# kv and kv with Wo per head on 32-column and 32 by 32 TensorE tiles, and Wo loaded in 8 pieces after the row of z

## The chip, the cores and the metric

One core of one Trainium2 chip (trn2). The metric is device time of one execution, in microseconds; the profile is one execution of the same kernel, and its span (829.4 us before) is a little shorter than the timed runs (830.83 us). All runs that are compared here are listed as fast in the record.

## The reference, cut to what matters

A transformer block with adaptive layer norm, linear attention (S = 2048, D = 1024, 32 heads of 32) and a gated feed-forward part.

```python
q, k, v = split_heads(h @ wqkv)                     # h: (2048, 1024), 32 heads of 32
pq, pk = phi(q), phi(k)
kv  = einsum('bhsd,bhse->bhde', pk, v)              # one 32 x 32 matrix per head
z   = einsum('bhsd->bhd', pk)
num = einsum('bhqd,bhde->bhqe', pq, kv)
den = einsum('bhqd,bhd->bhq', pq, z)[..., None] + 1e-06
x   = x + ga * ((num / den) @ wo)
# ... then layer norm and the feed-forward part, about 580 of the 830 us
```

The kernel reorders this. It forms `G = h^T pk` (h transposed times pk), then `kv = Wv^T G`, of which only the 32 by 32 block of each head on the diagonal counts, then `M = kv Wo` per head, and at the end one product of the scaled pq with M. The change touches kv, M and the load of Wo.

## The kernel before: the parts that matter

Tiles have fixed places in on-chip memory. Each engine runs its operations in the order in which they are recorded. All loads below go through the queue of SyncE ("SP"), also in order.

```python
P.dma("wo", WO[:], wov)                     # wov = A_wo as (kt p) n -> p kt n : one 2 MB load
G_BANKS = [0] + [next_bank() for _ in range(4)]         # five PSUM banks for the G groups

def z_row():                                # z as a row in DRAM, fetched back to all partitions (ZB)
    ...
    zw = P.dma("zw", ZDR..., ZR8[0:NHG, :])
    P.wait_for("sp", [zw])
    P.dma("zr", ZB[:], ZDR[0:1, :].to_broadcast([128, D]))

def den():                                  # denominators: 32 matmuls on 32-column tiles
    for hg in range(NHG):
        for ch in range(NCH):
            P.pe("matmul", out=PS[32*ch:32*ch+32, 7, :], lhsT=ZSEL[:, hg*32:hg*32+32], ...)
    ...                                     # reciprocal, written to DRAM (recip_den) in 4 stores,
    P.wait_for("sp", wr)                    # then 8 broadcast loads into RB, each 512 KB
    ...

def scale_pq(hg):                           # VectorE; waits for RB
    P.dve("tensor_tensor", out=PQT[:, hg, :], in0=PQT[:, hg, :], in1=RB[:, hg, :], op=ALU.mult)

def kvt_mm(half):                           # 32 matmuls 128x128, of each only the diagonal is kept
    for hl in range(4):
        hg = 4 * half + hl
        for dt in range(NDT):
            P.pe("matmul", out=PS[:, 6, hl*128:(hl+1)*128], lhsT=WV[:, dt, hg*128:(hg+1)*128],
                 rhs=G[:, dt, hg*128:(hg+1)*128], ...)
    P.dve("tensor_tensor", out=KVT[:, 4*half:4*half+4, :], in0=PS[:, 6, :]..., in1=MASK..., op=ALU.mult)

def m_mm(hg, banks):                        # 2 matmuls 128x512, evicted by ACT and DVE
    ...

for g in range(16):
    g_group(g)                              # 16 matmuls 128x512, 3.45 us
    ...                                     # g_evac: bank -> G (needs ZB); one group behind
    if g == 0: z_row()
    if g == 1: ...; den()
    if 6 <= g <= 9: ...                     # fold ga into WO (VectorE)
    if g == 10: kvt_mm(0)                   # needs the evictions of groups 0 to 7
    if 11 <= g < 15: m_mm(g - 11, [MB, 7])
    if 7 <= g < 15: scale_pq(g - 7)         # VectorE, in order with the evictions
    if g == 10: P.dma("stgx1", ...)         # 2 MB of w_mod
g_evac(15)
P.dma("stgx2", ...)                         # 2 MB of w_mod
...                                         # 4 + 3 reloads of x (xr0 .. xr6)
wo_part(0, 0, range(4)); wo_part(0, 1, range(2)); kvt_mm(1); wo_part(...); m_mm(4, ...); ...
for st in range(NST): ...                   # output projection with M (MW)
```

## Time and profile before

| | before |
|---|---|
| time, median of 4 | 830.83 us (830.82 to 831.24) |
| TensorE busy | 823.2 of 829.4 us |
| kv: 2 blocks of 32 matmuls 128x128 | 1.79 us each |
| kv with Wo: 16 matmuls 128x512 | 0.216 us each, 3.46 us |
| Wo load: issue, landing | 131.35 us, 9.2 us later |

The page's first part gives the busy time of each engine (PE is TensorE's matmuls, PEld its weight loads), its share of the span and the instruction count:

```profile
PE 823.2 (99%) x4083; PEld 378.8 (46%) x4083; DVE 312.6 (38%) x665; ACT 197.5 (24%) x336; POOL 39.9 (5%) x57
```

The timeline of PE in the stage of the change. Columns: start in us, duration from the first start to the last end, engine, line, operation, output and inputs, shape, count; a bracket at the end would name idle time and what ended it. Since matmuls overlap (a 128x512 one is listed with 0.379 us, and the next starts 0.216 us after it), the difference of two starts is the time a group really takes.

```profile
133.79 1.91 PE L176 MATMUL ps<-pqt,zsel 128*32 128x512 bf16 x32
135.63 31.25 PE L176 MATMUL ps<-pk,xres 128*128 128x512 bf16 x144
166.72 1.95 PE L176 MATMUL ps<-g,wv 128*128 128x128 bf16 x32
168.51 3.62 PE L176 MATMUL ps<-pk,xres 128*128 128x512 bf16 x16
171.96 0.59 PE L176 MATMUL ps<-wo,kvt 128*128 128x512 bf16 x2
...
187.50 1.46 PE L176 MATMUL ps<-mw,pqt 128*128 128x512 bf16 x6
188.80 1.95 PE L176 MATMUL ps<-g,wv 128*128 128x128 bf16 x32
...
194.47 5.78 PE L176 MATMUL ps<-mw,pqt 128*128 128x512 bf16 x26
```

No line has a bracket: PE never idles here. Read 168.51 - 166.72 = 1.79 us for a kv block (`ps<-g,wv`). The first line is the denominator step, already on 32-column tiles: 32 matmuls of 512 columns in 135.63 - 133.79 = 1.84 us, in rounds of four that start 3 to 4 ns apart, with 0.205 to 0.216 us to the next round, so four run at a time.

The timeline of SP's queue, the order in which transfers were issued (duration is that of the issuing, not of the transfer):

```profile
131.35 1.29 SPq L176 DMA_DIRECT2D wo<-in_A_wo_dram  x1
132.68 0.53 SPq L176 DMA_DIRECT2D z_row<-zr  x1
140.08 0.33 SPq L176 DMA_DIRECT2D zb<-z_row  x1
141.62 2.93 SPq L176 DMA_DIRECT2D recip_den<-rcb  x4
145.89 4.07 SPq L945 DMA_DIRECT2D rb<-recip_den  x8
```

The small store of z (4 KB) takes from 132.68 until its wait ends at 140.08 us, because 2 MB of Wo are on the way (in the changed kernel, without Wo ahead of it, from 131.02 to 133.77 us). The line of VectorE's timeline that receives rb, with the one after it:

```profile
157.77 1.23 DVE L176 TENSOR_TENSOR pqt<-pqt,rb 128x2048 bf16<-128x2048 bf16 x1 [2.71 <-DMA rb<-recip_den]
158.92 0.74 DVE L176 SCALAR_TENSOR_TENSOR g<-ps,modcol,gtmp 128x512 bf16<-128x512 f32 x1
```

VectorE waited 2.71 us for rb. It does its work in order, so the eviction of G's group 7 (copying the product G out of its PSUM bank), the next in its order, is held back by the same wait. It ends at 159.66 us and the kv block that needs it starts at 166.72 us, so seven microseconds are left.

### The profile page before, as it was taken

The page shows a single profiled execution, that of the slowest core. Times are in us where ns is not written, and L with a number is a line of the kernel's source. Part 1 is how long each engine was busy: PE and PEld are TensorE (multiplying, and loading weights), DVE is VectorE, ACT ScalarE, POOL GpSimd, SP SyncE. Part 2 cuts the span into 40 slices and gives each one's busy share as a digit, 9 for nine tenths or more (in the row PEclk, how much of TensorE's full clock was granted, in tenths as well). Part 3 has the DMA queues.
Part 4 walks back from the last instruction along what each step waited for, and adds up shares of the span by engine and source line. Part 5 has one row for each costly group of instructions (what it writes and reads, how often), then busy time and mean ns, then how long its engine had stood idle before and what let it go on. Part 6 is the DMA issues. An engine that isn't in the chain of part 4 may idle for free.

```text
span 829.4 us, 10017 instructions
## 1 busy us (share of the span) xinstructions
PE 823.2 (99%) x4083; PEld 378.8 (46%) x4083; DVE 312.6 (38%) x665; ACT 197.5 (24%) x336; POOL 39.9 (5%) x57
## 2 busy tenths in 40 slices
PE   8999999999999999999999999999999999999998
PEld 4544444444444444444444444444444444444444
DVE  5797986756955521121221112122111211221111
ACT  4757641323242111011111101111110111111011
POOL 1010000000130000030000003000000300000000
PEclk9999999999999999999999999999999999999999
DMA  9969656938397985700455571045557004553000
GB/s 321 287 151 231 148 159 171 201 104 304 60 256 229 276 264 158 192 25 15 124 155 150 153 185 33 16 124 153 154 151 190 26 18 123 154 152 87 0 26 26
DMA packets 199246, 119.28 MB, mean 144 GB/s; under 512 B 57881, under 2 KB 182945, under 8 KB 199201
## 3 DMA queue, kind: packets, MB, share of 16 engines
q1 hardware_dynamic: 199184, 118.65, 52.8%
q8 instruction: 32, 0.52, 0.3%
q14 instruction: 14, 0.11, 0.0%
q10 hardware_dynamic: 16, 0.00, 0.0%
HBM read 100.67 MB, written 4.33 MB: 127 GB/s over the span
## 4 chain that ended last, share of the span: by engine, by line
PE 97%; DMA 2%; SPq 1%; issue 0%; DVE 0%
PE ps L176 97%; DMA wsa<-in_w_mod_dram 2%; SPq L176 1%; DVE xres L176 0%
## 5 line engine op out<-in xcount | busy, mean ns | idle before, releaser
L176 PE MATMUL ps<-h2t,gug 128*128 128x512 bf16 x896 | 211.7, 379 | 0.0
L176 PE MATMUL ps<-h2t,guu 128*128 128x512 bf16 x896 | 211.7, 379 | 0.0
L176 DVE TENSOR_TENSOR at<-sg,ps 128x512 bf16<-128x512 bf16 x112 | 77.0, 687 | 282.8 <-PE ps L176 281.2
L176 ACT ACTIVATE sg<-ps 128x512 bf16<-128x512 f32 x112 | 66.9, 597 | 309.7 <-PE ps L176 309.7
L176 PEld LDWEIGHTS ps<-h2t,guu 128*128 128x128 bf16 x896 | 87.6, 98 | 105.7
L176 PEld LDWEIGHTS ps<-h2t,gug 128*128 128x128 bf16 x896 | 87.7, 98 | 105.5
L176 PE MATMUL ps<-wd_a,at 128*128 128x512 bf16 (+1 forms) x512 | 112.4, 377 | 0.0
L176 PE MATMUL ps<-ht,wqk 128*128 128x512 bf16 x512 | 111.7, 379 | 0.0
L176 PE MATMUL ps<-wd_b,at 128*128 128x512 bf16 (+1 forms) x384 | 85.0, 377 | 0.0
L176 PEld LDWEIGHTS ps<-wd_a,at 128*128 128x128 bf16 x512 | 50.1, 98 | 59.6
L176 DVE TENSOR_TENSOR ut<-att,gb_b 128x512 bf16<-128x512 bf16 (+1 forms) x32 | 14.3, 447 | 166.8 <-ACT att L176 166.8
L176 PEld LDWEIGHTS ps<-ht,wqk 128*128 128x128 bf16 x512 | 49.5, 98 | 58.7 <-DVE biasq L176 0.2
L176 ACT ACTIVATE att<-ps 128x512 bf16<-128x512 f32 (+1 forms) x32 | 17.4, 591 | 182.1 <-PE ps L176 182.1
L176 PEld LDWEIGHTS ps<-wd_b,at 128*128 128x128 bf16 x384 | 37.6, 98 | 44.7
L176 PE MATMUL ps<-pk,xres 128*128 128x512 bf16 x256 | 56.5, 379 | 0.0
L176 PE MATMUL ps<-mw,pqt 128*128 128x512 bf16 x256 | 56.3, 379 | 0.0
L176 POOL TENSOR_SCALAR h2t<-h2t,modcol 128x512 bf16<-128x512 bf16 x32 | 26.3, 836 | 383.4 <-DMA h2t<-xn 383.4
L176 ACT ACTIVATE e<-ps 128x512 bf16<-128x512 f32 x56 | 33.1, 603 | 31.7 <-PE ps L176 19.8
L176 PEld LDWEIGHTS ps<-mw,pqt 128*128 128x128 bf16 x256 | 24.9, 98 | 30.2 <-DVE xres L176 0.4
L176 PEld LDWEIGHTS ps<-pk,xres 128*128 128x128 bf16 x256 | 24.9, 98 | 29.9 <-issue 0.4
L176 ACT ACTIVATE junk<-xres 128x1024 bf16<-128x1024 bf16 x24 | 25.4, 1058 | 35.1 <-DVE xres L176 34.9
L176 DVE SCALAR_TENSOR_TENSOR xres<-ps,xres 128x512 bf16<-128x512 f32 x32 | 21.4, 688 | 12.3 <-PE ps L176 11.5
(107 smaller groups left out, 344.8 us busy)
## 6 DMA issues: line engine op xcount, KB each, us to landing
gug<-in_B_w_gate_dram SPq DMA_DIRECT2D x56, 512.0 KB, 4.0
guu<-in_B_w_up_dram SPq DMA_DIRECT2D x56, 512.0 KB, 5.3
xres<-in_A_x_dram SPq DMA_DIRECT2D x20, 256.0 KB, 7.7
rb<-recip_den SPq DMA_DIRECT2D x8, 512.0 KB, 11.5
stgx<-in_w_mod_dram SPq DMA_DIRECT2D x2, 2048.0 KB, 7.9
wd_a<-in_B_w_down_dram SPq DMA_DIRECT2D x4, 1024.0 KB, 7.8
out_dram<-xres SPq DMA_DIRECT2D x31, 128.0 KB, 1.7
xres<-in_A_x_dram SPq DMA_DIRECT2D x3, 1024.0 KB, 14.1
```

Source lines behind the costliest of these rows:

```text
L176: return getattr(e, method)(**kw)
```

## The change

Intent: of each 128 by 128 product only four 32 by 32 diagonal blocks are wanted. On 32-column tiles the four heads of a group are computed one beside the other, without the masked rest; for kv with Wo, sixteen 32 by 32 tiles work on sixteen heads at once (measured below: starts 3 to 4 ns apart in a round of four, and 2 to 5 ns apart for the sixteen). For the second step a head's kv sits on the partitions of its group `g`, and the kernel takes the rows of Wo from the same partitions, so they are reordered: row `(f g h e)` goes to partition `32 g + e`, slot `4 f + h`. One load per `(f, h)` does that, eight in all. They are issued after the fetch of the row of z, so that z no longer waits behind Wo.

```diff
-        KVT = T("kvt", 188 * KB, [128, NHG, 128], BF16)
+        KVT = T("kvt", 188 * KB, [128, 2, 128], BF16)
-        wov = A_wo.rearrange("(kt p) n -> p kt n", p=128)
+        wov = A_wo.rearrange("(f g h e) n -> f h g e n", f=2, g=4, h=4)
-        P.dma("wo", WO[:], wov)
         def kvt_mm(half):
-            for hl in range(4):
-                hg = 4 * half + hl
+            for h in range(4):
                 for dt in range(NDT):
-                    P.pe("matmul", out=PS[:, 6, hl * 128:(hl + 1) * 128], lhsT=WV[:, dt, hg * 128:(hg + 1) * 128],
-                         rhs=G[:, dt, hg * 128:(hg + 1) * 128], start=(hl == 0 and dt == 0), stop=(dt == NDT - 1),
+                    for g in range(4):
+                        c0 = 512 * half + 128 * g + 32 * h
+                        P.pe("matmul", out=PS[32 * g:32 * g + 32, 6, 32 * h:32 * h + 32], lhsT=WV[:, dt, c0:c0 + 32],
+                             rhs=G[:, dt, c0:c0 + 32], start=(h == 0 and dt == 0), stop=(dt == NDT - 1),
                          skip_group_check=True)
-            P.dve("tensor_tensor", out=KVT[:, 4 * half:4 * half + 4, :], ... MASK ...)
+            P.dve("tensor_copy", out=KVT[:, half, :], in_=PS[:, 6, 0:128])
-        def m_mm(hg, banks):  ...  # 2 matmuls 128x512
+        def m_mm(half, nh, banks):
+            for k in range(4):
+                for g in range(4):
+                    h = (g + k) % 4
+                    P.pe("matmul", out=PS[32 * h:32 * h + 32, banks[g], :],
+                         lhsT=KVT[32 * g:32 * g + 32, half, 32 * h:32 * h + 32],
+                         rhs=WO[32 * g:32 * g + 32, 4 * half + h, nh * 512:(nh + 1) * 512], start=True, stop=True,
+                         skip_group_check=True)
...                                           # four evictions per block, ACT and DVE in turn
             if g == 0:
                 z_row()
+                for f in range(2):
+                    for h in range(4):
+                        P.dma("wo%d%d" % (f, h), WO[:, 4 * f + h, :], wov[f, h])
...                                           # m_mm in 4 blocks instead of 8 pairs, banks, order of wo_part
```

More of the change, by code (lines that the diff above doesn't have):

```diff
@@ L904, in g_group @@
             h, dt = g // NDT, g % NDT
-            bank = G_BANKS[g % 5]
+            bank = G_BANKS[1 if g == 14 else g % 5]
             for st in range(NST):
@@ L911, in g_evac @@
             h, dt = g // NDT, g % NDT
-            bank = G_BANKS[g % 5]
+            bank = G_BANKS[1 if g == 14 else g % 5]
             i = g % 2
@@ L952, in kvt_mm @@
         def kvt_mm(half):
-            for hl in range(4):
-                hg = 4 * half + hl
+            for h in range(4):
                 for dt in range(NDT):
-                    P.pe("matmul", out=PS[:, 6, hl * 128:(hl + 1) * 128], lhsT=WV[:, dt, hg * 128:(hg + 1) * 128],
-                         rhs=G[:, dt, hg * 128:(hg + 1) * 128], start=(hl == 0 and dt == 0), stop=(dt == NDT - 1),
-                         skip_group_check=True)
-            P.dve("tensor_tensor", out=KVT[:, 4 * half:4 * half + 4, :],
-                  in0=PS[:, 6, :].rearrange("p (g d) -> p g d", g=4),
-                  in1=MASK[:].unsqueeze(1).to_broadcast([128, 4, 128]), op=ALU.mult)
@@ L963, in bass_adaLN_cond__linear_attn_block__swiglu_ffn__prompt_kernel @@
-        m_ctr = [0]
-        def m_mm(hg, banks):
-            for nh in range(2):
-                i = m_ctr[0]
-                m_ctr[0] += 1
-                bank = banks[i % len(banks)]
-                P.pe("matmul", out=PS[:, bank, :], lhsT=KVT[:, hg, :], rhs=WO[:, hg, nh * 512:(nh + 1) * 512],
-                     start=True, stop=True)
-                dst = MW[:, hg, nh * 512:(nh + 1) * 512]
-                if i % 2 == 0:
-                    P.act("activation", out=dst, in_=PS[:, bank, :], func=ACT.Copy)
+                    for g in range(4):
[3 more added lines that the diff above has]
+                             skip_group_check=True)
@@ new lines, in kvt_mm @@
+            P.dve("tensor_copy", out=KVT[:, half, :], in_=PS[:, 6, 0:128])
[6 more added lines that the diff above has]
+                         rhs=WO[32 * g:32 * g + 32, 4 * half + h, nh * 512:(nh + 1) * 512], start=True, stop=True,
+                         skip_group_check=True)
+            for g in range(4):
+                dst = MW[:, 4 * half + g, nh * 512:(nh + 1) * 512]
+                if g % 2 == 0:
+                    P.act("activation", out=dst, in_=PS[:, banks[g], :], func=ACT.Copy)
@@ L975, in m_mm @@
                 else:
-                    P.dve("tensor_copy", out=dst, in_=PS[:, bank, :])
+                    P.dve("tensor_copy", out=dst, in_=PS[:, banks[g], :])
         def fold_ga(jt):
@@ L1011, in bass_adaLN_cond__linear_attn_block__swiglu_ffn__prompt_kernel @@
                 kvt_mm(0)
-            if 11 <= g < 15:
-                m_mm(g - 11, [MB, 7])
+            if 11 <= g < 13:
+                m_mm(0, g - 11, [MB, 7, G_BANKS[4], 6])
             if 7 <= g < 15:
@@ L1025, in bass_adaLN_cond__linear_attn_block__swiglu_ffn__prompt_kernel @@
         wo_part(0, 1, range(2, 4))
-        wo_part(1, 0, range(3))
-        m_mm(4, [4, 5, 7, 6])
-        wo_part(1, 0, (3,))
-        wo_part(1, 1, (0,))
-        m_mm(5, [4, 5, 7, 6])
-        wo_part(1, 1, range(1, 3))
-        m_mm(6, [4, 5, 7, 6])
-        wo_part(1, 1, (3,))
-        m_mm(7, [4, 5, 7, 6])
+        wo_part(1, 0, range(1))
+        m_mm(1, 0, [4, 5, 7, 6])
+        wo_part(1, 0, range(1, 4))
+        wo_part(1, 1, range(4))
+        m_mm(1, 1, [4, 5, 7, 6])
         for ch in range(1, NCH):
@@ L1076, in bass_adaLN_cond__linear_attn_block__swiglu_ffn__prompt_kernel @@
         for st in range(NST):
-            for nh in range(2):
-                wo_part(st, nh, range(4, 8) if st < 2 else range(8))
-                wo_res(st, nh)
+            for (sw, nh) in (((0, 0), (1, 0)), ((0, 1), (1, 1)))[st] if st < 2 else ((st, 0), (st, 1)):
+                wo_part(sw, nh, range(4, 8) if st < 2 else range(8))
+                wo_res(sw, nh)
             if st >= 1:
```

## The prediction

> **What bounds it now.** TensorE. The page shows PE busy 823.2 of 829.4 us; the chain of waits that ended last is 97% PE. In the timeline of PE from 128 to 200 us no idle gap appears: a 128x512 matmul starts every 0.216 us, a 128x128 one every 0.056. Only PE work, or a new PE stall, can move the time; DVE (38%), ACT (24%) and DMA have slack.
>
> **What the change removes, adds, moves (128 to 200 us only).**
> 1. kv. Before: 2 blocks of 32 matmuls 128x128, 1.79 us each (timeline). After: 2 blocks of 128 matmuls on 32-column tiles, four at a time. The denominator step already runs in this mode: its start times show four 128x512 matmuls 3 to 4 ns apart, then 0.206 to 0.216 us to the next four, so four column tiles run together. The shortest spacing of weight load plus matmul on one tile here is 25 ns (the one-column matmuls at 10 to 27 us). 32 rounds of four give 0.8 us if tiles overlap as there; 3.2 us if instructions cannot pass faster than 25 ns per pair. The trace holds no long stream of short tiled matmuls: this is the weak term. Estimate: 1.2 us.
> 2. kv with Wo. Before: 16 full matmuls, 3.46 us. After: 4 blocks of 16 on 32 by 32 tiles. [...] nothing in this trace has 32-row tiles. Estimate per block: 0.216 + 16 x 4 ns = 0.28 us, against 0.86 before.
> 3. Mode switches. [...] into the denominator block the start gap is 0.309 us instead of 0.216, out of it 0.312; about 0.2 us the round trip. Six new blocks: 1.2 us.
> 4. VectorE: the masked 128x512 KVT product (0.69 us, twice) becomes a 128x128 copy. Off the chain, but PE awaits the second KVT, and only three matmuls (0.65 us) now stand behind the kv block instead of five. Reuse of the four banks between the last two Wo blocks is tight too (1.5 us of matmuls, about 1.5 us of evictions). Estimate 0.2 us of new stalls.
> 5. Wo loads. The row of z no longer queues behind 2 MB of Wo (zb landed at 144 us), so the G evictions start earlier; rb may land a little later (DVE waited 2.7 us for it). PE waited for neither before. Worth 0.
>
> **Sum.** kv: 2 x (1.2 - 1.79) = -1.2. Wo: 4 x (0.28 - 0.86) = -2.3. Switches +1.2, stalls +0.2. Total -2.1 us, all on the critical path: 830.83 becomes 828.8 us. Range 827.4 to 831.4. Faster by over 2%: 0.01; within: 0.98; slower: 0.01.
>
> **What would show each step.** PE timeline: a kv block of 0.8 to 1.5 us, starts of a round 4 ns apart; a Wo block of about 0.3 us; gaps of 0.3 us at each change of tile shape; no PE wait over 0.3 us on KVT, MW or banks; G evictions starting near 138 to 140 us; everything after 200 us only shifted.
>
> **What would make it wrong.** Instruction issue limits the short matmuls (a kv block of 2 us or more: gain gone). 32 by 32 tiles run four at a time, not 16 (a Wo block of 0.86 us: +2.3). [...] A late rb or Wo holding VectorE so long that G's banks come free late.

## More of the kernel before

A recording layer notes which operation reads and writes what and adds waits; it compares columns only, not partitions.

The reciprocals (`recip_den`) go out at 141.6 and rb from 145.9 us.

## The result, and the profile after

The changed kernel took 840.1 us (median of 4, 839.65 to 841.63) against 830.83 us, so it is 9.3 us slower; the ratio is 1.0114 (95% interval 1.0096 to 1.0131), inside the 2% that count as the same. Ratios here are the mean time of one kernel's fast runs over that of the other's fast runs of the same rounds, so they are not quite the ratio of the medians.

The page after, busy time first: PE did a little less work in a longer span.

```profile
PE 822.5 (98%) x4323; PEld 376.7 (45%) x4323; DVE 310.9 (37%) x665; ACT 197.4 (24%) x336; POOL 39.9 (5%) x57
```

PE's timeline of the same stage:

```profile
135.32 31.25 PE L176 MATMUL ps<-pk,xres 128*128 128x512 bf16 x144
166.50 0.38 PE L176 MATMUL ps<-g,wv 128*32 128x32 bf16 x28
173.46 0.99 PE L176 MATMUL ps<-g,wv 128*32 128x32 bf16 x100 [6.58 <-DVE g L176]
174.38 5.10 PE L176 MATMUL ps<-pk,xres 128*128 128x512 bf16 x16
179.56 0.44 PE L176 MATMUL ps<-wo,kvt 32*32 32x512 bf16 x16
179.93 1.04 PE L176 MATMUL ps<-pk,xres 128*128 128x512 bf16 x4
182.65 2.75 PE L176 MATMUL ps<-pk,xres 128*128 128x512 bf16 x12 [1.69 <-issue]
...
196.07 1.46 PE L176 MATMUL ps<-mw,pqt 128*128 128x512 bf16 x6
197.46 1.19 PE L176 MATMUL ps<-g,wv 128*32 128x32 bf16 x128
...
201.69 1.04 PE L176 MATMUL ps<-mw,pqt 128*128 128x512 bf16 x4
203.81 11.38 PE L176 MATMUL ps<-mw,pqt 128*128 128x512 bf16 x52 [1.09 <-issue]
```

Three gaps are new. The first, 6.58 us in the middle of the first kv block, ends with an eviction of G by VectorE. The 16 matmuls after it take 5.1 us instead of 3.6: the first eight start 0.40 to 0.43 us apart. The other two gaps have the releaser "issue", which means that no semaphore explains them. The tiled blocks themselves are short, as intended.

Followed back from the first gap, the chain leads to the queue of loads. SP's timeline:

```profile
131.02 1.21 SPq L176 DMA_DIRECT2D z_row<-zr  x1
...
134.15 13.36 SPq L176 DMA_DIRECT2D wo<-in_A_wo_dram  x8
147.56 3.91 SPq L176 DMA_DIRECT2D recip_den<-rcb  x4
159.61 4.04 SPq L944 DMA_DIRECT2D rb<-recip_den  x8
```

Issuing the eight Wo loads took 13.36 us. The reciprocals went out at 147.56 instead of 141.62 us, and were confirmed 12 us later instead of 4, so rb started at 159.6 instead of 145.9 us. VectorE shows what that did:

```profile
171.43 1.23 DVE L176 TENSOR_TENSOR pqt<-pqt,rb 128x2048 bf16<-128x2048 bf16 x1 [16.68 <-DMA rb<-recip_den]
172.57 0.75 DVE L176 SCALAR_TENSOR_TENSOR g<-ps,modcol,gtmp 128x512 bf16<-128x512 f32 x1
```

It sat 16.68 us in front of `scale_pq(0)`, and the eviction of G's group 7, next in its order, came at 172.57 instead of 158.92 us. PE's kv block wanted it at 166.7 us.

Why the loads were slow is seen in two stretches of the windows view of the changed kernel (columns: stretch in us; its length; busy time and number of instructions on PE, PEld, DVE, ACT, POOL; granted clock; mean busy share of the 16 DMA engines; GB/s):

```profile
134.00:148.00 14.00, 14.00 (x87) 6.25 (x80) 10.24 (x12) 4.81 (x7) 0.00 (x0) 1.00 0.31 115
148.00:160.00 12.00, 12.00 (x58) 5.45 (x56) 3.90 (x6) 1.44 (x2) 0.00 (x0) 1.00 0.26 97
```

While Wo was loading, the mean busy share was about a quarter and the engines moved about 100 GB/s. The trace's semaphore updates say the same: each of the changed kernel's Wo loads reported five times, one update at issue and four as data landed, while the one load of before reported sixteen times. Four landings and a share of 0.26 of the 16 engines (4 of 16 would be 0.25) say that a load ran on four of them. The slowest dimension of these loads is `g`, of size 4; that of the load of before is `p`, of size 128. That its size sets the number of engines is the author's estimate from these two; experiment 1 adds a load with 32 there.

The reciprocals' updates show who was waiting for whom. The first of their four stores reported twelve landings at 150.95 to 151.12 us, about 1 us after its issue ended, and the last four only at 158.53 to 159.00 us, each 0.2 us after one of the four landings of the last Wo load (158.35 to 158.83). So three quarters of that store were through at once, and by these times the last quarter stood behind Wo.

### Where the 8.8 us of this stage went

From the two timelines, as differences of start times:

| term | us |
|---|---|
| gap inside the first kv block (starts at 166.69 and 173.46) | +6.76 |
| matmuls at half clock afterwards (8 matmuls in 3.21 instead of 1.73, 174.38 to 177.59) | +1.48 |
| "issue" gap at 182.65 (2.07 between starts instead of 0.216) | +1.85 |
| "issue" gap at 203.81 (1.47 instead of 0.216) | +1.25 |
| longer wait for KVT before the first Wo block | +0.15 |
| what is left: the tiled blocks themselves | -2.70 |
| measured for the stage: (203.81 - 135.32) - (195.33 - 135.63) | +8.79 |

(195.33 is the kernel before at the same point, four matmuls after 194.47.) The last term is a remainder, not a measurement, and needs its own test: if it is right, the tiles are worth 2.7 us once the gaps are gone.

The half clock is in the windows view too: the granted clock was 1.00 in the first 3.6 us of the gap (166.88 to 170.50 us), 0.51 from 170.50 to 177.40, and 1.00 from there to 200. So in this run the clock fell some 3.6 us into the gap of 6.6 us and was back some 3.9 us after PE resumed at 173.46.

### The profile page after: what moved, and what is told of

Same layout as the page of the kernel before. It is cut to its first block, busy times and chain, and to the rows that moved or that the text cites. A ratio compares the mean times of both kernels' runs of the same rounds, so it can differ in the third digit from the quotient of the medians.

```text
span 837.8 us, 10508 instructions
## 1 busy us (share of the span) xinstructions
PE 822.5 (98%) x4323; PEld 376.7 (45%) x4323; DVE 310.9 (37%) x665; ACT 197.4 (24%) x336; POOL 39.9 (5%) x57
## 4 chain that ended last, share of the span: by engine, by line
PE 87%; DVE 5%; DMA 4%; SPq 2%; issue 1%; ACT 0%; DVEq 0%; ACTq 0%
PE ps L176 87%; DVE acc L176 2%; SPq L176 2%; DMA rb<-recip_den 1%; DMA stg<-in_w_mod_dram 1%; DMA recip_den<-rcb 1%; DVE pqt L176 1%; DVE pkt L176 1%; DVE e L176 1%; DMA xres<-in_A_x_dram 0%; DVE mhl L176 0%; DMA z_row<-zr 0%; DVE wo L176 0%; DVE g L176 0%; DVE stats L176 0%
## 5 line engine op out<-in xcount | busy, mean ns | idle before, releaser
L176 PEld LDWEIGHTS ps<-mw,pqt 128*128 128x128 bf16 x256 | 24.7, 98 | 31.4 <-issue 1.8
## 6 DMA issues: line engine op xcount, KB each, us to landing
xres<-in_A_x_dram SPq DMA_DIRECT2D x3, 1024.0 KB, 13.7
```

The lines of the kernel that those rows point to most:

```text
L176: return getattr(e, method)(**kw)
```

## The experiments

Theory A: the loss is the Wo load on 4 DMA engines, which holds back the reciprocals and rb, then VectorE, then PE. Rival B: eight loads at this place are bad however they are cut. Rival C: the tiled matmuls, their banks or changes of mode hold PE.

### 1. Wo cut by 32 partitions, in the changed kernel

```diff
-        wov = A_wo.rearrange("(f g h e) n -> f h g e n", f=2, g=4, h=4)
+        wov = A_wo.rearrange("(f g h e) n -> f g e h n", f=2, g=4, h=4)
-                        P.dma("wo%d%d" % (f, h), WO[:, 4 * f + h, :], wov[f, h])
+                        P.dma("wo%d%d" % (f, h), WO[32 * h:32 * h + 32, 4 * f:4 * f + 4, :], wov[f, h])
```

> The changed kernel, with its 8 loads of Wo (256 KB each, 2 KB rows, same place in the queue) cut by groups of 32 partitions, so that the slowest dimension of a load is 32 instead of 4. Theory A (a load whose slowest dimension is 4 runs on 4 of the 16 DMA engines, at 101 GB/s as the trace shows, and the write of the reciprocals queues behind it): each Wo load is issued in about 0.5 us instead of 1.7, Wo lands by 146 us, the reciprocals land by 147 us instead of 159.5, rb's first half by 159 us, VectorE waits under 4 us for rb instead of 16.7, PE has no 6.6 us stall before the first kv block; time 827.5 to 831. Rival B (any 8 loads at this place delay the chain) and rival C (the tiled matmuls or their banks hold PE): time stays at 838 or more. If the two instruction-fetch gaps of 1.7 and 1.1 us are there by themselves, at least one stays, and the time is nearer 831.

Measured: 839.43 us (before in the same rounds 831.20; ratio 1.0098), correct. This looks like a refutation of theory A, and it is a failed experiment instead. SP's timeline:

```profile
135.59 20.89 SPq L176 DMA_DIRECT2D wo<-in_A_wo_dram  x8
156.52 1.82 SPq L176 DMA_DIRECT2D recip_den<-rcb  x4
```

Each load now reported 16 landings, so the 16 engines were used, and a load was through about 3 us after its issue. But six of the eight were issued only when the one before had landed: SP's list of waits has 18.0 us, in six waits, for Wo itself. Loads to partitions 0 to 31 and 32 to 63 of the same columns look like overlapping writes to the recording layer, which compares columns only, and it chained them. The reciprocals left at 156.5 us, later still, and rb began at 159.9 us, as in the changed kernel, with the same loss (gap of 5.3 us in the first kv block). What it does show is that the loss follows the time at which the reciprocals are through, whatever holds them back.

### 2. The kernel before with eight late loads, and with the 4-row loads

Eight loads of 128 rows in the old layout, issued at the changed kernel's place:

```diff
-        P.dma("wo", WO[:], wov)
             if g == 0:
                 z_row()
+                for i in range(NHG):
+                    P.dma("wo%d" % i, WO[:, i, :], wov[:, i, :])
```

> The kernel before with its one load of Wo replaced by 8 loads of 128 rows in its own layout (slowest dimension 128), issued where the changed kernel issues them, after the fetch of the row of z. Theory A: harmless, 830.5 to 831.5 us, no PE stall; rb at most 2 us later than before. Rival B: 836 us or more.

Measured: 831.52 us against 831.20 (ratio 1.0002, 0.9987 to 1.0017). The eight issues took 4.20 us and the reciprocals left at 140.59 us, so eight loads at this place need not hurt. Rival B falls.

The same with `wov = A_wo.rearrange("(f g h e) n -> f h g e n", ...)`, so the loads of the changed kernel under the matmuls of before (the result is wrong in its values, not in the amount of work):

> Wrong result on purpose (rows of Wo in the changed kernel's order under the matmuls of before). The kernel before, with the changed kernel's 8 loads of Wo (slowest dimension 4) at the changed kernel's place, and all matmuls of before. Theory A: the loss appears without any tiled matmul: Wo loads 2.5 us apart, reciprocals landed at about 159 us, PE stalled some 6 to 7 us before the first kv block, then slow clock; time 838 to 840 us. Rival C (tiled matmuls): 831 us.

Measured: 839.99 us against 831.20 (ratio 1.0107, 1.0092 to 1.0122). (The comparison with the reference doesn't see an attention term with permuted rows; the time is what counts here.) SP and PE:

```profile
134.51 13.98 SPq L176 DMA_DIRECT2D wo<-in_A_wo_dram  x8
```

```profile
174.20 2.80 PE L176 MATMUL ps<-g,wv 128*128 128x128 bf16 x25 [6.88 <-DVE g L176]
```

The whole gap appears without a single new tile. Rival C falls for this gap: the layout of the loads alone makes it.

### 3. Wo cut by 32 partitions, not chained

Four loads are recorded as one operation, so nothing is put between them:

```diff
+                    outs = [WO[32 * g_:32 * g_ + 32, 4 * f:4 * f + 4, :] for g_ in range(4)]
+                    ins = [wov[f, g_] for g_ in range(4)]
+                    def fn(e, outs=outs, ins=ins):
+                        return [e.dma_start(out=o_, in_=i_) for o_, i_ in zip(outs, ins)]
+                    P.add("sp", fn, reads=[], writes=outs, lane="wo%d" % f, ninc=4, tag="wo")
```

> The cut by 32 partitions again. In the run before it each load waited for the one before to land, because the recording layer takes loads to different partitions of the same columns for overlapping; here four loads go out as one operation, so they are not chained. Theory A (what delays the reciprocals is that Wo occupies the queue and its engines until about 159 us; on 16 engines and unchained it is gone by 145 us): reciprocals landed by 147 us, rb's halves at 151 and 161 us, no PE stall of 5 to 7 us before the first kv block; time 827.5 to 831, the lower end if the two fetch gaps (1.7 and 1.1 us) vanish too, since the rb traffic is over by then, the upper end if they stay. If time stays at 838 or more, theory A is wrong and the tiled blocks themselves are to blame.

Measured: 830.26 us against 831.06 (ratio 0.9987, 0.9970 to 1.0004). About ten microseconds came back from cutting the same 2 MB of Wo differently. SP's queue:

```profile
134.90 4.54 SPq L1006 DMA_DIRECT2D wo<-in_A_wo_dram  x8
141.74 1.71 SPq L176 DMA_DIRECT2D recip_den<-rcb  x4
150.30 4.19 SPq L944 DMA_DIRECT2D rb<-recip_den  x8
```

Rb started 4 us later than before but early enough: VectorE waited 6.74 us for it, and PE didn't wait. Two times of the expectation were missed by some 3 us: Wo landed at 148.63 us, not 145, and the reciprocals at 150.22, not 147. PE:

```profile
186.79 1.46 PE L176 MATMUL ps<-mw,pqt 128*128 128x512 bf16 x6
188.18 1.19 PE L176 MATMUL ps<-g,wv 128*32 128x32 bf16 x128
189.30 0.82 PE L176 MATMUL ps<-mw,pqt 128*128 128x512 bf16 x3
190.06 0.43 PE L176 MATMUL ps<-wo,kvt 32*32 32x512 bf16 x16
190.42 1.68 PE L176 MATMUL ps<-mw,pqt 128*128 128x512 bf16 x7
...
192.40 1.04 PE L176 MATMUL ps<-mw,pqt 128*128 128x512 bf16 x4
195.09 20.23 PE L176 MATMUL ps<-mw,pqt 128*128 128x512 bf16 x93 [1.65 <-issue]
```

Here the tiles can be priced. The second kv block costs 189.30 - 186.79 less six matmuls of 0.216, so 1.21 us with both changes of mode (before: 1.79). A Wo block costs 190.42 - 189.30 less three matmuls, so 0.47 us with its changes of mode (before: 0.86). Together 2 x 0.58 + 4 x 0.39 = 2.7 us, the remainder of the balance above. But one of the "issue" gaps is still there and eats 1.65 us of it (the profile is of the slowest of the four runs, 830.93 us).

### 4. What the "issue" gap is

The trace shows the packets that bring instructions: one of 16,384 bytes for each 256 instructions of PE (32 packets for 8,166 matmuls and weight loads in the kernel before, 34 for 8,646 in the changed one). In the feed-forward part, from 298 us on, these packets start when PE is at number 152 to 172 of each 256 in the trace's order in the kernel before, and at 153 to 180 in the changed one. The "issue" gaps lie at numbers 2241 and 2753 in the changed kernel and at 2753 in the version of experiment 3, so at number 193 of a 256. That suggested theory F: these are edges of instruction blocks; a block is asked for when the one before it is entered; the request waits behind data traffic; and a kv block, which is 256 instructions in 1.1 us instead of the 28 us that 256 take at 0.216 us per pair, uses up the lead. Times around the gaps (from PE's instruction numbers and the packets' start times; "due" is the author's estimate, worked out from the edge one block before, since the trace shows the packets but no requests):

| version | edge | due | packet starts | PE runs on at |
|---|---|---|---|---|
| changed kernel | 2241 | about 173.5 | 179.91 | 182.65 |
| changed kernel | 2753 | about 197.8 | 201.35 | 203.81 |
| experiment 3 | 2753 | about 188.5 | 192.73 | 195.09 |

A packet takes 1.0 to 1.3 us and PE ran on 2.4 to 2.7 us after its start. Rival G: PE waits there for a bank, an eviction or the reload of x, and the profile misses the semaphore.

Three versions of experiment 3 and a control, on one chip. First, 144 more PE instructions at the start and nothing else, which moves all block edges against the program:

```diff
-        warm(13, bank=3)                  # 13 warm-up matmuls of 512 columns
+        warm(85, bank=3, w=64)            # 85 of 64 columns
```

> The kernel of the run before (Wo cut by 32 partitions, unchained; 830.26 us, one PE gap of 1.65 us left after the last Wo block), with its 13 warm-up matmuls of 512 columns at the start replaced by 85 of 64 columns: 144 more PE instructions ahead of everything, about the same warm-up time, no change in dependences. Theory F (the gap is PE out of instructions: they come in blocks of 256, a block is asked for when the one before it is entered, the request waits 3 to 5 us behind DMA traffic, and a kv block of 256 instructions is eaten in 1.2 us): the block edge moves from just behind the last Wo block to inside the second kv block, with the next one 60 matmuls later, so the gap vanishes and the time falls by about 1.6 us, to 828.3 to 829.2. Rival G (PE waits there for a bank, an eviction or the reload of x): gap and time stay.

Second, the same with `warm(49, bank=3, w=128)`, 72 more instructions:

> The same with 49 warm-up matmuls of 128 columns: 72 more PE instructions. Theory F: the block edge falls into the first of the two late Wo blocks; the block is asked for at about 186 us, in full traffic; so the gap moves ahead by some 3 us to a place inside or next to that Wo block, and is 1 to 3 us long; time 829.5 to 831.5. Rival G: the gap stays where it was, behind the last Wo block, at 1.65 us.

Third, no shift, but less traffic around the second kv block:

```diff
-        P.dma("stgx2", STGX[1][:], wmv[:, :, 5120:6144])          # was before the reloads of x
+        P.wait_for("sp", [P.by_eng["pe"][-1]])                    # last Wo block, ahead of xr4 .. xr6
         for ch in range(1, NCH):
             P.dma("xr%d" % (3 + ch), XRES[:, 4*ch:4*ch+4, :], xv[:, 4*ch:4*ch+4, :])
...
             if st == 6:
                 macc_split()
+                P.dma("stgx2", STGX[1][:], wmv[:, :, 5120:6144])
```

> The same kernel without the shift; instead the second 2 MB load of w_mod is issued some 30 us later, and the three 1 MB reloads of x wait for the last Wo block, so that DMA is nearly idle when the second kv block runs (four 256 KB reloads remain, done by 187 us). Theory F: the request at about 188.5 us is served at once, the block is there by 191 us, no gap; time 828.3 to 829.2. Rival G in its form 'PE waits for x or a bank': the gap stays or grows, time 830 or more.

And the control, the kernel before with those two moves of loads:

> Control: the kernel before, with the same two moves of loads. It has no such gap, so nothing is to be gained: 830.5 to 831.3 us.

| version | median, us | ratio to before (831.41) | gap after the last Wo block |
|---|---|---|---|
| 144 instructions more | 829.65 | 0.9981 (0.9969 to 0.9994) | none |
| 72 instructions more | 833.23 | 1.0022 (1.0008 to 1.0035) | moved |
| less traffic | 828.85 | 0.9971 (0.9958 to 0.9983) | none |
| control | 831.21 | 0.9999 (0.9987 to 1.0012) | none |

With 72 more instructions PE's timeline reads:

```profile
171.59 3.40 PE L176 MATMUL ps<-pk,xres 128*128 128x512 bf16 x15 [2.84 <-issue]
...
192.85 0.40 PE L176 MATMUL ps<-wo,kvt 32*32 32x512 bf16 x7
194.19 0.41 PE L176 MATMUL ps<-wo,kvt 32*32 32x512 bf16 x9 [0.94 <-issue]
```

The gap moved into the middle of a Wo block, between its seventh and eighth matmul, where no operand or bank could be awaited that the others had not had. A second gap, of 2.84 us, opened behind the first kv block; the expectation had overlooked that the shift puts an edge there too, in the middle of the rb traffic, and so missed the time by 1.7 us. With 144 more, both edges lie in harmless places and there is no gap. That version's median didn't reach the 828.3 to 829.2 us expected. In its profile the start went slower: the granted clock was 0.50 from 9.40 to 12.80 us, where experiment 3 had 1.00, and the first large products (`ht,wqk`) began at 14.04 instead of 12.07 us. But this profile is of its slowest run (830.62 us, the only one of five with a mean clock below 1.000), so what kept the other four back isn't known.

With less traffic, the windows of 188 to 193 us compare as follows, experiment 3 first:

```profile
188.00:193.00 5.00, 5.00 (x175) 2.49 (x174) 1.99 (x4) 1.53 (x3) 0.00 (x0) 1.00 1.06 390
```

and the version with less traffic, with PE's line behind its last Wo block, which has no bracket:

```profile
188.00:193.00 5.00, 4.84 (x173) 2.49 (x171) 2.27 (x5) 1.80 (x4) 0.00 (x0) 1.00 0.04 12
192.13 23.05 PE L176 MATMUL ps<-mw,pqt 128*128 128x512 bf16 x104
```

The DMA engines went from full to idle, the instruction packet started at 189.22 instead of 192.73 us, and the gap was gone; both later runs with less traffic (section 5) have no such gap either. Position and traffic move the gap as theory F says, and PE's waits were the same in the two shifted versions; rival G falls. It is the traces that carry this, not the times: experiment 3 was not run again beside these versions, and its ratio (0.9987, 0.9970 to 1.0004) overlaps those of the two faster ones. The version with less traffic also shows the lead. There PE passed the edge at 193.0 us (192.13 plus four matmuls) without a stop while a packet was still on its way (192.59 to 193.68), so that packet held a later block, and the one that begins at the edge had come before. The control shows that the moved loads are worth nothing by themselves. Not settled: why a fetch is held up by traffic for 3.5 to 6.4 us. It was in the three cases of the table, and no run here takes that apart.

### 5. The place of the loads alone

The best version (less traffic) with Wo loaded where the kernel before loads it, ahead of the row of z, beside its partner:

> The best kernel so far (tiled matmuls, Wo cut by 32 partitions and unchained, less traffic at the second kv block; 828.85 us) with its Wo loads issued where the kernel before issues its one load, ahead of the row of z. This undoes the move alone. The prediction's 'worth 0' for the move: the row of z lands later again (G evictions begin near 145 us instead of 138), the reciprocals and rb somewhat earlier, PE waits for neither; 828.3 to 829.4 us, no difference from its partner beyond noise. If the move matters, 830 or more.

> Its partner again, on the same chip: 828.3 to 829.4 us, 2 to 2.6 us under the kernel before.

Measured: 833.48 us (831.52 to 834.24) for the early loads and 829.04 us for the partner, before 831.21. The expectation was wrong. The profiled run is the fastest of the five; its queue and PE:

```profile
131.35 4.87 SPq L903 DMA_DIRECT2D wo<-in_A_wo_dram  x8
136.27 0.33 SPq L176 DMA_DIRECT2D z_row<-zr  x1
143.52 0.36 SPq L176 DMA_DIRECT2D zb<-z_row  x1
```

```profile
148.92 20.89 PE L176 MATMUL ps<-pk,xres 128*128 128x512 bf16 x96 [2.61 <-DVE g L176]
```

Eight issues take 4.87 us where one took 1.29, and the store of z is issued 3.6 us later. This cut of Wo also lands more slowly, 12.0 us after the first issue instead of 9.2; which of the two holds z back isn't separated. The row of z is back at 147.3 instead of 144.0 us, the first eviction of G at 148.1 instead of 144.9, and the sixth group of G, which reuses the first bank, waits 2.61 us. In the kernel before, that bank was free at about 145.6 us (144.87 plus one eviction) and wanted at 146.0: a slack of 0.4 us that no list of waits shows, since nobody waited. So with Wo in these eight loads, the move behind z is needed. The four other runs took 1.9 to 2.7 us more, and they list a mean granted clock of 0.998 where the profiled one has 1.000. Over 830 us that is about 1.7 us (an estimate from these two figures), so a stretch at half clock, such as the 3.4 us at 0.50 in the profile with 144 more instructions, would explain most of it, but no profile of such a run was kept.

Not tried: Wo on tiles with kv on full matmuls. It would have fewer instructions, and would need every fourth group of 32 columns as the stationary operand.

## Why the prediction was right or wrong

- **What bounds the kernel, and that only PE work or a new PE stall counts: right.** The balance of the stage closes on PE alone.
- **kv on column tiles (1.2 us plus 0.2 for the switches): close.** Measured 1.21 us with the switches. In experiment 3 the first 32 matmuls run in rounds, starts 3 to 4 ns apart and 15 ns to the next round; from then on they start one by one every 8 to 9 ns. The fear that issue would limit them at 25 ns per pair was unfounded; 8 to 9 ns is the spacing that shows. Neither of the two cases that the prediction weighed (0.8 us and 3.2 us) describes this stream, and its 1.2 us was a guess between them, so that it came out close is luck.
- **kv with Wo on 16 tiles (0.28 us plus 0.2): right.** Measured 0.47 us. In experiment 3 the 16 starts are 2 to 5 ns apart, and the last ends 0.43 us after the first starts, so all sixteen tiles run together. Since the trace of before had no 32-row tiles, this was the author's estimate, with the 3 to 4 ns of the denominator step as the spacing.
- **"Switches +1.2, stalls +0.2", sum -2.1 us: right in the end.** The version without the two obstacles measured 2.56 us (831.41 to 828.85) and 2.17 us (831.21 to 829.04) below before.
- **"Wo loads ... rb may land a little later ... Worth 0": this is the step that failed.** It measured +8.2 us (6.8 of gap and 1.5 of slow clock). The prediction counted the loads as 2 MB in either case and looked at their place in the queue, but not at their shape. The slowest dimension was `g` = 4 in the line of the diff, and each load had four landings instead of sixteen. The chain it then named as harmless, reciprocals to rb to VectorE to G to PE, is the one that broke: rb was not "a little" but 13.7 us late, against some 7 us of slack. The last sentence of the prediction lists this as a risk ("a late rb or Wo holding VectorE so long that G's banks come free late") without costing it; even there it was the kv operand rather than a bank that PE missed.
- **Instruction fetch: absent from the prediction**, which spoke of instruction issue as a rate only. It cost 1.85 and 1.25 us in the changed kernel, and 1.65 us after the load was mended.
- **The move: right that the G evictions start earlier, wrong that it is worth nothing.** The first eviction came at 140.85 instead of 144.87 us, and the kernel before had no use for it. But the eight loads at the old place cost 2.6 us of PE.

## What to carry to other kernels

When a diff rearranges a load, read its outermost dimension before its bytes: with 4 there, 2 MB took 24.7 us (134.15 to 158.83) instead of 9.2 with 128, and the stores of the reciprocals queued behind it were through 12 us after the first was issued, instead of 4. Follow what stands behind such a load in its queue to the engine it feeds, and compare its delay with the slack there; slack is the difference between when a thing was ready and when it was wanted, and the list of waits is silent about it. Replacing a few large instructions by many small ones saved array time here (0.58 us per kv block, 0.39 per Wo block) but spent instruction supply (gaps of 0.9 to 2.8 us, and none after the last Wo block when the DMA share was 0.04): keep such a burst away from heavy DMA traffic, or check where the 256-instruction edges fall.

## What else the traces show of the hardware

- Narrow loads (5 updates per load, 4 of them landings; share 0.26 to 0.31, 97 to 115 GB/s) also held up the issuing queue: from the fifth load on, each issue itself took 2.5 to 3.0 us instead of the 0.5 to 0.7 of the first four, so 13.4 us for eight, and the 32 KB stores behind them were confirmed 12 us after the first issue instead of 4.
- By theory F, PE ran dry at block edges for 0.9 to 2.8 us, with one block of lead as far as the runs show. In the three cases of the table a kv block of short instructions (256 in 1.1 us in the second block) had met DMA engines at a share of 1.0 (1.01 at 173.46 to 174.38 us and 1.05 at 197.46 to 198.59 in the changed kernel, 1.06 at 188 to 193 in experiment 3), and the packet started 3.5 to 6.4 us after it was due.
- On one tile most of the one-column matmuls start 25 ns apart (111 of the 128 with `siluc` in the kernel before). With four column tiles in turn the last 96 starts of 128x32 matmuls, with their weight loads, in the changed kernel's second kv block came 8.4 ns apart on average.
- A change of mode takes about 0.1 us each way (start gaps of 0.31 instead of 0.216 us, into and out of the denominator step of the kernel before and the Wo block at 199.34 us of the changed one).
